# Turning the output weights for the router with six transposing DMAs instead of TensorE transposes

## The chip, the cores and the metric

The kernel runs on one core of a Trainium2 chip. The metric is the time of one execution in microseconds of the device. Three runs of the kernel before gave 1300.38, 1301.32 and 1308.1 us; the median, 1301.32 us, is the time before.

## What is computed

The reference is an attention between tokens and a small state, a gated MLP on its result, and a top-1 mixture of eight experts on the result of that. Cut to what matters:

```python
a  = softmax(scale * x @ state^T);   xread = a @ state      # per batch b (8) and head (8)
a2 = softmax(scale * state @ x^T);   sread = a2 @ x
x  = concat(xread, sread)                                   # 8 x (512 + 32) = 4352 rows of 512
h  = sigmoid(x @ w_gate) * (x @ w_val)                      # 512 -> 1536
x  = h @ w_out                                              # 1536 -> 512
logits = x @ moe2_w_gate                                    # 512 -> 8
e = argmax(logits); p = softmax(logits)[e]
out = p * relu(x @ w1[e]) @ w2[e]                           # 512 -> 1024 -> 512
```

The first three weights come as float64, which the kernel turns into float32 with integer operations; every product of two matrices is made of three float16 matmuls over high and low parts.

## The kernel before

The token rows of the first MLP are worked off in eight blocks of 512 tokens, one for each batch b (`token_block`), then come the 256 state rows, then the expert tiles of 128 rows (37 of them, `expert_tile`, L826), for which each row goes to its expert's list in DRAM. The hidden width of 1536 is cut into twelve groups of 128 (fc = 0 to 11, `NFC`), or six pairs (`NFP`).

In a block the work has two parts. First twelve steps of `gate_val` make the hidden activations (L618 to L620). Then four output rounds, j = 0 to 3, one for 128 tokens each (`mlp_out`, L669), add up twelve groups of three matmuls of 128x512 (L674 to L676) with the output weights `wout[:, fc, l]` (l = 1 the high, l = 0 the low part). At fc = 3, at fc = 7 and at its end a round calls `mid()`, which runs what a table has for that numbered slot: 25, 26, 27 are those of round 0, 28 to 30 of round 1, 31 to 33 of round 2, 34 to 36 of round 3. In these slots stand pieces of the next block's attention (L317 transposes, L330, L349, L390, L397, L408), of its state weights (L440, six times, in every second slot, copied out by ScalarE at L447 and VectorE at L448) and, in block 0 only, `router_weights`, in slots 25 to 31 and 33. Behind each slot a step of a background queue runs.

The router does not read the rows of the MLP's result. It multiplies the hidden activations with `gw`, which is w_out times the router's weights, made once in block 0: `gsum` (L979), its maximum (L985), then `gw` (L991, L992). For that product the output weights have to be turned, so that the 512 columns of a group lie on the partitions.

The output weights are ready late. `conv_wout` scales them group by group in block 0: ScalarE rounds a group into a buffer `junk`, VectorE writes the low part (L293, called at L546) and copies the high part (L547). The buffers `junk`, `wt`, `g` and `ls` share one pair of buffers (tag "g" of `tmp`).

The large buffers (`big`, five of 4 KB per partition) hold the raw output weights (twelve loads, L514), then the expert weights (L565). `conv_experts` takes these as 64 parts of 512 KB: each is loaded, its absolute maximum taken (by VectorE at L581 for w1, by ScalarE at L585 for w2), and eight parts later it is loaded again, scaled, split and written back to DRAM (L592). Input loads are L256 and L207. All of them are issued by SyncE (SP).

TensorE's order is that in which the code is written; in this part of the program the orders of the other engines and of SP come from a scheduler. Each engine, and SP's queue, works off its list in order, and waits at an instruction whose operands or buffers aren't ready. A buffer is given to a new tile when its last reader is done.

Of the kernel before, what the change touches and what calls it, by code (L numbers as in the profile page):

```python
# [10 lines left out]
F16 = mybir.dt.float16  # L11
I32 = mybir.dt.int32
AF = mybir.ActivationFunctionType
ALU = mybir.AluOpType
AX = mybir.AxisListType
# [3 lines left out]
P = 128  # L19
# [6 lines left out]
def attention_moe_router_kernel(  # L26
# [24 lines left out]
    nc = tc.nc  # L51
# [5 lines left out]
    NE, _, F2 = w1.shape  # L57
    NDC = DM // P
    NFC = DF // P
# [26 lines left out]
    NFP = NFC // 2  # L86
# [12 lines left out]
    ident = const.tile([P, P], F16, name="ident", tag="ident")  # L99
# [17 lines left out]
    g2p = const.tile([P, NDC, 2 * NE], F16, name="g2p", tag="g2p")  # L117
    gsum = const.tile([P, NFC, NE], F32, name="gsum", tag="gsum")
# [4 lines left out]
    def tl(shape, dt=F32, name="t", bufs=None, pool=None):  # L123
        kw = {} if bufs is None else {"bufs": bufs}
        return (pool or tiny).tile(shape, dt, name=name, tag=name, **kw)

    def pow2_scale(m, k, nm, lim=40, inv=True, bufs=None):

        n = m.shape[1]
        a = tl([P, n], I32, nm + "a")  # L130
        s = tl([P, n], I32, nm + "s", bufs)
        nc.vector.tensor_scalar(a, m.bitcast(I32), EXPO, EXPO, ALU.bitwise_and, ALU.bitwise_xor)
        nc.vector.tensor_scalar(
            s, a, float((128 + lim) * ONE), float((k - 1) * ONE), ALU.min, ALU.add
        )
        if not inv:
            return s.bitcast(F32), None
        c = tl([P, n], I32, nm + "c", bufs)
        nc.vector.tensor_scalar(c, s, -1.0, float(254 * ONE), ALU.mult, ALU.add)
        return s.bitcast(F32), c.bitcast(F32)  # L140
# [21 lines left out]
    tmp = mlp.enter_context(tc.tile_pool(name="tmp", bufs=2))  # L162
    big_p = mlp.enter_context(tc.tile_pool(name="big_p", bufs=5))
# [5 lines left out]
    wout = wpool.tile([P, NFC, 2, DM], F16, name="wout", tag="wout")  # L169
    x1s = wpool.tile([P, NDC, B * NS], F32, name="x1s", tag="x1s")  # L170

    def at_ps(shape, dt=F32):
        return at_p.tile(shape, dt, name="at", tag="at")
# [4 lines left out]
    def spread(m):  # L178

        n = m.shape[1]  # L180
        ps = at_ps([P, n, P])
        for i in range(n):
            nc.tensor.matmul(
                ps[:, i], m[:, i:i + 1].to_broadcast([P, P]), identf, start=True, stop=True
            )
        return ps

    def all_max(ps, nm):
        r = tl([P, ps.shape[1]], name=nm)
        nc.vector.tensor_reduce(r, ps, axis=AX.X, op=ALU.max)  # L190
        return r
# [92 lines left out]
    def pair(v, h16, l16, s=None, inplace=False):  # L284

        if inplace:
            nc.scalar.activation(v, v, AF.Copy, scale=s)  # L287
        if s is None or inplace:
            nc.scalar.copy(h16, v)  # L289
            nc.gpsimd.tensor_tensor(l16, v, h16, op=ALU.subtract)  # L290
        else:
            nc.scalar.activation(h16, v, AF.Copy, scale=s)
            nc.vector.scalar_tensor_tensor(l16, v, s, h16, op0=ALU.mult, op1=ALU.subtract)  # L293
# [661 lines left out]
    def router_weights():  # L955

        wt = {}
        for k in range(NFC + 1):
            if k < NFC:
                pt = at_ps([P, 2, NDC, P], F16)  # L960
                for l in range(2):
                    for c in range(NDC):
                        nc.tensor.transpose(
                            pt[:, l, c], wout[:, k, 1 - l, c * P:(c + 1) * P], ident
                        )
                wt[k] = tmp.tile([P, 2, NDC, P], F16, name="wt", tag="g")
                nc.vector.tensor_copy(wt[k], pt)
            if k > 0:
                pg = at_ps([P, 2, NE])
                w = wt.pop(k - 1)  # L970
                for c in range(NDC):
                    nc.tensor.matmul(
                        pg.rearrange("p l e -> p (l e)"), w[:, 0, c], g2p[:, c],
                        start=(c == 0), stop=False,
                    )
                    nc.tensor.matmul(
                        pg[:, 0], w[:, 1, c], g2p[:, c, 0:NE], start=False, stop=(c == NDC - 1)
                    )
                nc.vector.tensor_reduce(  # L979
                    gsum[:, k - 1], pg.rearrange("p l e -> p e l"), axis=AX.X, op=ALU.add  # L980
                )
            if k % 2 == 1:
                yield
        m = tl([P, 1], name="gm")
        nc.vector.tensor_reduce(  # L985
            m, gsum.rearrange("p f e -> p (f e)"), axis=AX.X, op=ALU.max, apply_absolute_value=True
        )
        yield
        r = all_max(spread(m), "gr")
        s, i = pow2_scale(r, 14, "gs")  # L990
        pair(gsum, gw[:, :, 0, 0], gw[:, :, 0, 1], s)  # L991
        nc.vector.tensor_copy(gw[:, :, 1, 0], gw[:, :, 0, 0])  # L992
        nc.vector.tensor_tensor(inv_g, inv_g, i, op=ALU.mult)
        yield
# [30 lines left out]
    def token_block(b):  # L1025
# [36 lines left out]
        if b == 0:  # L1062

            rw = router_weights()
            for slot in (25, 26, 27, 28, 29, 30, 31, 33):
                at(slot, lambda: next(rw, None))
# [102 lines left out]
    n = B * NS  # L1169
# [181 lines left out]
```

## Time and profile before

| | before |
|---|---|
| median of three runs | 1301.32 us |
| profiled execution: run, span | 1309.01 us, 1307.2 us |
| TensorE busy, share of the span | 1142.4 us, 87% |
| VectorE, ScalarE, GpSimd busy | 816.9, 589.8, 331.3 us |
| mean granted TensorE clock | 0.936 |
| router weights: first transpose, first matmul of block 1 | 174.76 us, 238.04 us |

The times of a trace count from the start of its span. A row of the order of time gives start, duration, engine, source line, operation, output and input tiles, and in brackets how long the engine had been idle and who ended that. The rows that matter stand below.

### The profile page before, as it was taken

What the parts mean: (1) busy time and instruction counts of PE and PEld (TensorE: products, weight loads), DVE (VectorE), ACT (ScalarE), POOL (GpSimd) and SP (SyncE); (2) the same over time, 40 slices, a digit from 0 to 9 for tenths busy, and PEclk for the clock granted to TensorE, in tenths of its full rate; (3) what the DMA queues carried; (4) which work ended last, traced back from release to release, by engine and by line L of the source; (5) the groups of instructions that cost most, each with busy time, mean ns of one, the idle gap of its engine ahead of it and who ended that gap; (6) DMA issues with size and microseconds to landing.
All of it is one profiled execution on the core that took longest, in us unless ns stands there. A gap on an engine that the chain in (4) does not pass through costs nothing.

```text
span 1307.2 us, 23292 instructions
## 1 busy us (share of the span) xinstructions
PE 1142.4 (87%) x8855; PEld 644.1 (49%) x8855; DVE 816.9 (62%) x1918; ACT 589.8 (45%) x963; POOL 331.3 (25%) x273
## 2 busy tenths in 40 slices
PE   3366659889889899799899999999999999999995
PEld 2222225444344444334444444486777766666773
DVE  7778877677768678686767574333644444444442
ACT  3666652576585785686785744121111111111110
POOL 1253200233252451351540714131110000000110
PEclk9577779899899999899899999999999999999998
DMA  7404420185576766476765300027322277879347
GB/s 249 165 33 146 161 85 6 48 276 182 194 242 217 258 224 252 162 255 228 267 212 187 122 2 34 1 105 229 125 60 62 53 243 237 290 198 383 89 122 230
DMA packets 118803, 216.71 MB, mean 166 GB/s; under 512 B 61215, under 2 KB 69407, under 8 KB 115360
## 3 DMA queue, kind: packets, MB, share of 16 engines
q1 hardware_dynamic: 113008, 197.07, 45.5%
q0 software_dynamic: 5680, 18.11, 3.6%
q8 instruction: 72, 1.18, 0.4%
q14 instruction: 43, 0.35, 0.1%
HBM read 259.35 MB, written 54.88 MB: 240 GB/s over the span
## 4 chain that ended last, share of the span: by engine, by line
PE 45%; DVE 18%; DMA 15%; ACT 12%; issue 6%; SPq 3%; POOL 1%; POOLq 0%; DVEq 0%; ACTq 0%
DMA big<-in_moe_w_dram 10%; PE mm L836 9%; PE mm L839 4%; PE mm L857 4%; PE mm L858 4%; PE mm L856 4%; PE mm L620 3%; PE mm L618 3%; PE mm L619 3%; PE mm L674 3%; PE mm L675 3%; PE mm L676 3%; DMA out_dram<-g,meta 2%; ACT big L287 2%; ACT big L585 1%
## 5 line engine op out<-in xcount | busy, mean ns | idle before, releaser
L850 ACT ACTIVATE acth<-v 128x256 f16<-128x256 f32 x148 | 61.8, 417 | 323.9 <-DVE v L849 302.3
L836 PE MATMUL mm<-big,wgv 128*128 128x256 f16 x1184 | 199.3, 273 | 0.4 <-DMA wgv<-w_d 0.4
L839 PE MATMUL mm<-big,wgv 128*128 128x128 f16 x1184 | 197.4, 219 | 0.0
L618 PE MATMUL mm<-aT,M 128*128 128x512 f16 x384 | 156.7, 408 | 42.0 <-ACT M L447 22.5
L631 POOL TENSOR_TENSOR actl<-g,acth 128x512 f16<-128x512 f32 (+1 forms) x108 | 127.7, 1185 | 181.2 <-ACT acth L630 180.5
L620 PE MATMUL mm<-aT,M 128*128 128x512 f16 x384 | 156.7, 408 | 13.2 <-DVE M L448 7.5
L674 PE MATMUL mm<-wout,acth 128*128 128x512 f16 x408 | 159.6, 391 | 8.8 <-DVE wout L547 6.8
L675 PE MATMUL mm<-wout,acth 128*128 128x512 f16 x408 | 158.9, 389 | 0.0
L676 PE MATMUL mm<-wout,actl 128*128 128x512 f16 x408 | 158.5, 389 | 0.0
L619 PE MATMUL mm<-aT,M 128*128 128x512 f16 x384 | 156.7, 408 | 0.0
L625 DVE SCALAR_TENSOR_TENSOR g<-mm,g 128x512 f32<-128x512 f32 (+1 forms) x108 | 70.9, 658 | 88.4 <-PE mm L620 42.0
L836 PEld LDWEIGHTS <-wgv 128*128 128x128 f16 x1184 | 115.8, 98 | 18.2 <-DMA wgv<-w_d 0.9
L864 POOL DMA_INDIRECT out_dram<-g,meta x37 | 36.2, 978 | 341.5 <-DVE g L861 304.5
L839 PEld LDWEIGHTS <-wgv 128*128 128x128 f16 x1184 | 115.8, 98 | 4.0
L849 DVE TENSOR_REDUCE v<-mm 128x256 f32<-128x512 f32 x148 | 101.4, 686 | 19.2 <-PE mm L839 18.2
L851 DVE SCALAR_TENSOR_TENSOR actl<-v,acth 128x256 f16<-128x256 f32 x148 | 62.9, 425 | 69.9 <-ACT acth L850 66.8
L290 POOL TENSOR_TENSOR big<-big 128x1024 f16<-128x1024 f32 x32 | 68.2, 2131 | 108.5 <-ACT big L289 96.5
L776 POOL DMA_INDIRECT rows_d<-xrow,rri x34 | 36.4, 1070 | 215.8 <-DVE kg L715 64.9
L630 ACT CAST acth<-g 128x512 f16<-128x512 f32 (+1 forms) x108 | 63.8, 591 | 53.0 <-DVE g L625 52.8
L861 DVE TENSOR_SCALAR g<-mm,meta,slot_inv 128x512 f32<-128x512 f32 x33 | 26.7, 810 | 95.6 <-PE mm L858 95.6
L624 ACT ACTIVATE g<-mm,sgf 128x512 f32<-128x512 f32 (+1 forms) x108 | 71.0, 659 | 24.6 <-PE mm L620 22.1
L448 DVE SCALAR_TENSOR_TENSOR M<-mm,M 128x512 f16<-128x512 f32 x96 | 62.5, 683 | 22.6 <-ACT M L447 22.6
(297 smaller groups left out, 2183.8 us busy)
## 6 DMA issues: line engine op xcount, KB each, us to landing
wgv<-w_d SPq DMA_DIRECT2D x59, 2048.0 KB
big<-in_moe_w_dram SPq DMA_DIRECT2D x128, 512.0 KB
wout<-w_d SPq DMA_DIRECT2D x19, 2048.0 KB
w_d<-big SPq DMA_DIRECT2D x64, 512.0 KB
xb<-in_x_dram SPq DMA_DIRECT2D x60, 128.0 KB
big<-in_moe_w_out_dram SPq DMA_DIRECT2D x12, 512.0 KB
wgv<-in_moe_w_gate_dram SPq DMA_DIRECT2D x3, 1024.0 KB
wgv<-in_moe_w_val_dram SPq DMA_DIRECT2D x3, 1024.0 KB
```

The source lines that it names most:

```text
L618: nc.tensor.matmul(ps[k], w[0], v[0], start=(i == 0), stop=False)
L619: nc.tensor.matmul(ps[k], w[0], v[1], start=False, stop=False)
L620: nc.tensor.matmul(ps[k], w[1], v[0], start=False, stop=(i == len(parts) - 1))
L624: mark["sig"] = nc.scalar.activation(g, ps[0], AF.Sigmoid, scale=sg[:, fc:fc + 1])
L625: nc.vector.scalar_tensor_tensor(g, ps[1], 2.0 ** -v_sh, g, op0=ALU.mult, op1=ALU.mult)
L631: nc.gpsimd.tensor_tensor(lo, g, h, op=ALU.subtract)
L674: nc.tensor.matmul(po, hj, wout[:, fc, 1], start=(fc == 0), stop=False)
L675: nc.tensor.matmul(po, hj, wout[:, fc, 0], start=False, stop=False)
L676: nc.tensor.matmul(po, lj, wout[:, fc, 1], start=False, stop=(fc == NFC - 1))
L836: nc.tensor.matmul(ph[:, i], w1s[:, c, 0, f:f + P], t[:, :, c], start=(c == 0), stop=False)
L839: nc.tensor.matmul(ph[:, i, 1], w1s[:, c, 1, f:f + P], t[:, 0, c], start=False, stop=(c == NDC - 1),)
L849: nc.vector.tensor_reduce(v, ph.rearrange("p i l q -> p i q l"), axis=AX.X, op=ALU.add)
```

## The change

The transposes on TensorE, their copies out of PSUM by VectorE and the tiles `wt` in the pair of "g" buffers are taken out. In their place six DMAs, issued by SP, each turn a pair of groups with both parts (128 partitions by 2048 float16, 512 KB) from `wout` into a large buffer. Two are issued in slot 25, one more ahead of each of the next four pairs; the router matmuls read the large buffers directly. The matmuls and the sums of the product stay as they were (new lines L976, L980 for L972, L976, and L983 for L979); those of pair n stand in slot 26 + n, where before the first group's stood in slot 25.

```diff
     def router_weights():
 
         wt = {}
-        for k in range(NFC + 1):
-            if k < NFC:
-                pt = at_ps([P, 2, NDC, P], F16)
-                for l in range(2):
-                    for c in range(NDC):
-                        nc.tensor.transpose(
-                            pt[:, l, c], wout[:, k, 1 - l, c * P:(c + 1) * P], ident
-                        )
-                wt[k] = tmp.tile([P, 2, NDC, P], F16, name="wt", tag="g")
-                nc.vector.tensor_copy(wt[k], pt)
-            if k > 0:
+
+        def turn(m):
+            if m < NFP:
+                wt[m] = big_p.tile([P, 2, 2, NDC, P], F16, name="big", tag="big")
+                nc.sync.dma_start_transpose(
+                    out=wt[m].rearrange("p k l c f -> p (k l c) f"),
+                    in_=wout[:, 2 * m:2 * m + 2].rearrange("p k l d -> p (k l d)"),
+                )
+
+        turn(0)
+        turn(1)
+        yield
+        for n in range(NFP):
+            turn(n + 2)
+            for i in range(2):
                 pg = at_ps([P, 2, NE])
-                w = wt.pop(k - 1)
+                w = wt[n][:, i]
...
-            if k % 2 == 1:
+            if n < NFP - 1:
                 yield
```

On TensorE, in round 0 behind fc 3, the transposes L963 of two groups and the router matmuls of the first group (`wt` is the copied transpose, `g2p` the router's weights) stood between an attention transpose and the matmuls of fc 4. Before:

```order
L317 MATMUL at<-ident,xn 128x128
L963 LDWEIGHTS wout
L963 MATMUL at<-ident,wout 128x128
...
L972 LDWEIGHTS wt
L972 MATMUL at<-g2p,wt 128x16
L976 LDWEIGHTS wt
L976 MATMUL at<-g2p,wt 128x8
...
L674 LDWEIGHTS acth
L674 MATMUL mm<-wout,acth 128x512
```

Now the same place, down to the router matmuls of the first pair, which read a large buffer and stand behind fc 7 and the state weights:

```order
L317 MATMUL at<-ident,xn 128x128
L674 LDWEIGHTS acth
L674 MATMUL mm<-wout,acth 128x512
...
L440 LDWEIGHTS bdT
L440 MATMUL mm<-wgv,bdT 32x512
...
L976 LDWEIGHTS big
L976 MATMUL at<-g2p,big 128x16
```

The sixteen transposes and eight router matmuls left the place; fc 4 follows the attention transposes directly.

On SP, behind the twelve loads of the raw output weights (`in_moe_w_dram` are the expert weights, `in_x_dram` and `in_state_dram` inputs):

```order
 L514 DMA big<-in_moe_w_out_dram 128x1024 x12
-L565 DMA big<-in_moe_w_dram 128x1024
-L256 DMA xb<-in_x_dram 128x256 x4
-L565 DMA big<-in_moe_w_dram 128x1024 x3
-L565 DMA big<-in_moe_w_dram 128x2x512
-L256 DMA xb<-in_x_dram 128x256 x4
+L256 DMA xb<-in_x_dram 128x256 x8
+L962 DMA_TRANSPOSE big<-wout 128x16x128 x2
+L565 DMA big<-in_moe_w_dram 128x1024
+L962 DMA_TRANSPOSE big<-wout 128x16x128
+L565 DMA big<-in_moe_w_dram 128x1024
+L962 DMA_TRANSPOSE big<-wout 128x16x128 x3
```

The first five expert loads stood ahead of the second input load; now two stand between the transposing DMAs and the third behind the last of them.

On VectorE, at the end of the conversions (L293 and L547 write `wout`; `gsum` is the router product, `em` an expert maximum):

```order
 L547 COPY wout<-junk 128x512
 L293 SCALAR_TENSOR_TENSOR wout<-wout,osc,junk 128x512
-L967 COPY wt<-at 128x1024
+L983 TENSOR_REDUCE gsum<-at 128x8
+L448 SCALAR_TENSOR_TENSOR M<-mm,M 128x512
 L547 COPY wout<-junk 128x512
-L581 TENSOR_REDUCE em<-big 128x1 x4
-L967 COPY wt<-at 128x1024
-L979 TENSOR_REDUCE gsum<-at 128x8
-L601 TENSOR_REDUCE ea<-em 128x1 x2
```

Ahead of the last conversion's copy a sum of the router product and a state weight copy have taken the place of a `wt` copy, and the four expert maxima that followed it are spread out behind.

## Rows read from the trace of the kernel before

**Rows 1.** The page: span and TensorE's busy time, share and instructions.
```profile
span 1307.2 us, 23292 instructions
PE 1142.4 (87%) x8855; PEld 644.1 (49%) x8855; DVE 816.9 (62%) x1918; ACT 589.8 (45%) x963; POOL 331.3 (25%) x273
```
**Rows 2.** Stages: length, busy us of PE, PEld, DVE, ACT, POOL; granted clock, DMA, GB/s.
```profile
174.96:181.91 6.95, 0.86 (x16) 0.68 (x13) 6.78 (x14) 5.12 (x8) 0.00 (x0) 0.91 0.00 0
...
192.00:238.04 46.04, 42.83 (x487) 23.57 (x484) 32.05 (x91) 13.20 (x24) 2.52 (x2) 1.00 0.02 5
...
173.90:180.70 6.80, 1.92 (x33) 1.74 (x31) 5.57 (x12) 5.34 (x8) 0.00 (x0) 1.00 0.00 0
180.70:187.50 6.80, 5.58 (x28) 2.00 (x36) 6.61 (x10) 1.92 (x4) 0.00 (x0) 0.50 0.64 199
```
**Rows 3.** PE's waits, 160 to 245 us: total us, times, longest us.
```profile
PE at L972 <- DVE wt L967: 11.5, 4, 6.1
```
**Rows 4.** PE in order of time: start, us, line, tiles, count, idle before.
```profile
174.76 1.06 PE L963 MATMUL at<-ident,wout 128*128 128x128 f16 x16
181.91 0.19 PE L972 MATMUL at<-g2p,wt 128*128 128x16 f16 x1 [6.10 <-DVE wt L967]
...
182.15 0.59 PE L674 MATMUL mm<-wout,acth 128*128 128x512 f16 x1
...
187.36 0.90 PE L440 MATMUL mm<-wgv,bdT 64*32 64x512 f16 x24
188.19 0.62 PE L963 MATMUL at<-ident,wout 128*128 128x128 f16 x8
188.65 0.17 PE L972 MATMUL at<-g2p,wt 128*128 128x16 f16 x1
...
191.78 0.18 PE L972 MATMUL at<-g2p,wt 128*128 128x16 f16 x1 [2.33 <-DVE wt L967]
...
192.00 0.38 PE L674 MATMUL mm<-wout,acth 128*128 128x512 f16 x1
192.21 0.38 PE L675 MATMUL mm<-wout,acth 128*128 128x512 f16 x1
...
209.25 0.18 PE L972 MATMUL at<-g2p,wt 128*128 128x16 f16 x1 [2.36 <-DVE wt L967]
...
238.04 0.38 PE L618 MATMUL mm<-aT,M 128*128 128x512 f16 x1
```
**Rows 5.** DVE in order of time, at the end of the conversions.
```profile
177.34 0.29 DVE L547 COPY wout<-junk 128x512 f16<-128x512 f16 x1
...
181.18 0.68 DVE L967 COPY wt<-at 128x1024 f16<-128x1024 f16 x1
181.78 0.28 DVE L547 COPY wout<-junk 128x512 f16<-128x512 f16 x1
```
**Rows 6.** SP's queue in order of time, and the stage of the expert loads.
```profile
181.49 5.54 SPq L565 DMA_DIRECT2D big<-in_moe_w_dram  x5
187.12 26.99 SPq L207 DMA_DIRECT2D st<-in_state_dram  x16
242.15 18.52 SPq L256 DMA_DIRECT2D xb<-in_x_dram  x8
...
181.00:191.00 10.00, 7.54 (x68) 3.20 (x68) 6.34 (x11) 3.98 (x9) 0.00 (x0) 0.67 0.78 252
```
**Rows 7.** L819: ns of one on SP (least, median, most); one of them; its stage.
```profile
L819 SPq DMA_TRANSPOSE big<-rows_d x41: 1242/1269/7444, 875.2 to 1294.4; - x41
...
939.93 1.27 SPq L819 DMA_TRANSPOSE big<-rows_d  x1
...
940.00:943.00 3.00, 3.00 (x27) 1.97 (x25) 2.23 (x5) 0.99 (x3) 0.00 (x0) 1.00 0.44 90
```
**Rows 8.** The chain of waits in order of time: two expert loads, start and us.
```profile
399.36 4.19 DMA big<-in_moe_w_dram
...
638.89 8.18 DMA big<-in_moe_w_dram
```

More of the change, by code (lines that the diff above doesn't have):

```diff
@@ L957, in router_weights @@
         wt = {}
-        for k in range(NFC + 1):
-            if k < NFC:
-                pt = at_ps([P, 2, NDC, P], F16)
-                for l in range(2):
-                    for c in range(NDC):
-                        nc.tensor.transpose(
-                            pt[:, l, c], wout[:, k, 1 - l, c * P:(c + 1) * P], ident
-                        )
-                wt[k] = tmp.tile([P, 2, NDC, P], F16, name="wt", tag="g")
-                nc.vector.tensor_copy(wt[k], pt)
-            if k > 0:
+        def turn(m):
[11 more added lines that the diff above has]
+            for i in range(2):
                 pg = at_ps([P, 2, NE])
-                w = wt.pop(k - 1)
+                w = wt[n][:, i]
                 for c in range(NDC):
                     nc.tensor.matmul(
-                        pg.rearrange("p l e -> p (l e)"), w[:, 0, c], g2p[:, c],
+                        pg.rearrange("p l e -> p (l e)"), w[:, 1, c], g2p[:, c],
                         start=(c == 0), stop=False,
@@ L976, in router_weights @@
                     nc.tensor.matmul(
-                        pg[:, 0], w[:, 1, c], g2p[:, c, 0:NE], start=False, stop=(c == NDC - 1)
+                        pg[:, 0], w[:, 0, c], g2p[:, c, 0:NE], start=False, stop=(c == NDC - 1)
                     )
                 nc.vector.tensor_reduce(
-                    gsum[:, k - 1], pg.rearrange("p l e -> p e l"), axis=AX.X, op=ALU.add
+                    gsum[:, 2 * n + i], pg.rearrange("p l e -> p e l"), axis=AX.X, op=ALU.add
                 )
-            if k % 2 == 1:
+            if n < NFP - 1:
                 yield
```

## The prediction

> **What bounds the kernel now.** I read the page first: TensorE (PE) is busy 87% of a span of 1307.2 us [rows 1], so a change that only empties another engine gives nothing, and I looked for the stretch that the diff touches and for what ended PE's waits in it. The router weights are made in block 0, in its four output rounds (j = 0 to 3, twelve groups fc of three matmuls each), from the first transpose at 174.76 us to the first matmul of block 1 at 238.04 us [rows 4]. The table by stage shows PE nearly idle at first (0.86 us busy of 6.95) while VectorE (DVE) is full (6.78 of 6.95), and a granted clock that goes 1.00, then 0.50 after the idle time [rows 2]. The table of waits names the cause: PE waited 11.5 us in four places at L972 for DVE's copy L967 [rows 3]. The longest is 6.1 us. DVE's order shows why: the copy L967 at 181.18 stands behind the conversions of the output weights (L293, L547; L547 of group 7 is at 177.34, that of the last group at 181.78, so about 1.1 us for each) [rows 5]. The next waits are the same kind: 2.33 us until 191.78 and 2.36 us until 209.25 [rows 4], the copy being behind DVE instructions that themselves wait (the expert maxima L581, then a maximum that waits for ScalarE, which waits for expert loads).
>
> **The sum: what goes.** All of it is measured against the profiled execution (span 1307.2, run 1309.01 us); the median of the three runs, 1301.32, is 7.7 us lower, and as this stretch is early and short, I subtract the same microseconds from the median.
> - 96 transposes leave PE. Eight of them take 0.62 us with the last one's tail, and the next instruction starts 0.46 us after the first (188.19 and 188.65, [rows 4]); twelve eights are 5.5 us.
> - The four waits for L967: 11.5 us [rows 3].
> - The half clock. Between 182.15 and 187.36 the twelve matmuls of fc 4 to 7 take 0.43 us each; at 192.00 and 192.21 the same matmul takes 0.215 [rows 4]. The clock had been granted at 1.00 from 173.9 and fell at 180.7, after PE had stood idle for 4.9 of 6.8 us [rows 2]. Without that idle time I expect it to stay up: 2.6 us.
>
> Together 19.6 us, which I take as the most that can be won; twelve copies of 0.68 us [rows 5] leave DVE too, but DVE is only worth what PE waits for it.
>
> **The walk: what is in the way instead.** With the transposes gone, fc 4 of round 0 starts at 174.96. It now meets the conversions themselves: fc 6 and fc 7 need their L547, and the one at 177.34 (group 7) ends at 177.63 [rows 5]. So fc 7 ends near 178.3; then the 24 matmuls L440 (0.8) and the first router pair (0.4, both from the starts in rows 4) bring fc 8 to 179.5, against 192.00: 12.5 us ahead. The last conversion gets a little later, because the new order puts two L983 and one L448 ahead of its L547 and these wait for PE and ScalarE: I put its end at 182.4 instead of 182.06, so fc 11 waits 0.9 us. Then rounds 1 to 3 save eight more transpose groups (8 x 0.46 = 3.7) and two waits (2.36 [rows 4] and what is left of the 11.5 after 6.1, 2.33 and 2.36, 0.7): 3.1 us. 12.5 - 0.9 + 3.7 + 3.1 = 18.4 us.
>
> **The six DMAs.** They wait on SP for their pair of groups and for a buffer, and SP is free for them: its next work before was the five expert loads at 181.49 [rows 6], and ahead of the transposes stand input loads alone. No transpose out of on-chip memory is in the trace. The nearest rows are the 41 transposes of L819, out of DRAM and half as large (128x1024): median 1.27 us on SP, one of 7.44 at worst [rows 7]; in the three microseconds from 940.00, which begin with one issued at 939.93, 90 GB/s or 270 KB went by, that is all of its 256 KB. Doubled, 2.5 us of SP each, and my estimate is that they land 4 us (lower bound 3.1, as for the half size) after the start. I take the median, as the same operation with the same piece size (16 rows by 128) is issued. Pair 0 is issued at about 169, needed at 179; pair 5 is needed at about 200, and six in a row from 169 with T = 2.5 are through long before. In detail pairs 3, 4 and 5 wait for buffers: for the first pair to be used (179.5), for the first L581 (184) and for the second pair (184.4), so they are issued by 189.2 and are 8 us early or more. With T up to 4.8 us ((200 - 169 - 2) / 6) nothing is late.
>
> Behind them on SP stand the expert loads of block 0. Five were resident before the conversions ended and five more were issued from 181.49 [rows 6]; now only two are ahead, and the third is issued at about 189.6, when pair 5 is out. A load that the chain waited for took 4.19 us [rows 8], so it lands near 193.6; DVE asks for it (L581) near 192.5 and behind it stand the row maxima L680 and L685 of round 1, for which a later L440 waits. So about 1 us of DVE is late, which this stretch can swallow (DVE was busy 32.05 of the last 46.04 us [rows 2]), and the next loads come one after another. By the first matmul of block 1 SP must have caught up: before, its row of state loads ended at 214.11 (187.12 and 26.99) and the next input load went out at 242.15 [rows 6], so the lag is inside its slack. From block 1 on, the order of every engine is the same as before and the rest should be moved as one piece.
>
> I subtract 3.4 us from the 18.4 for what a walk leaves out: one stretch of half clock somewhere else (2.6, as above) and 0.8 for late expert loads. **15 us** are left: 1301.3 - 15 = 1286.3.
>
> **The rivals.**
> - *Loads late, part of the gain given back.* The longest load that the chain waited for took 8.18 us [rows 8]. If the third to eighth load of block 0 take 8 us instead of 4, DVE and ScalarE stand 4 us at each of two places in their order, with L685 and the copies L447 behind: 4 to 8 us back, 1290 to 1298, say 1293. For it: the loads now queue behind six transposes. Against it: the five that were queued together at 181.49 went by within the ten microseconds to 191, at 252 GB/s [rows 6], 2 us each.
> - *The gain is lost later.* Blocks 1 to 7 also wait for expert loads, and if the loads set their pace, an earlier start buys nothing: 1301, within 4 us. Against it: SP's idle stretch before 242.15 says that the loads wait for PE's progress there and not the other way round.
> - *Slow transposes (the other side).* SBUF as the source may be slower than DRAM. The place is the wait of the router matmuls in PE's fixed order; each microsecond of T over 4.8 costs 6 us, as six stand in a row, so at T = 7.3 the gain is gone. At twice the worst row, T = 14.9, the cost is 6 x 10.1 - 15 = 46 us: 1347. For it: no row shows this source. Against: the median of 41 rows. The Trainium skill speaks for this rival ("VectorE: DVE Perf Modes", section "The three transpose paths"): it gives 1309 ns for one 128x128 block through the DMA against 390 ns on TensorE, and advises TensorE where the result may go to PSUM. By that figure, as an estimate, a DMA of sixteen blocks takes 20.9 us and the kernel 6 x 16.1 - 15 = 82 us more. The trace does not agree for the DRAM source: eight blocks took 1.27 us of SP [rows 7], where the page's figure would make 10.5.
>
> **How the numbers follow.** The forecast, 12 to 20 us won, gets 0.60; late loads 0.22; gain lost later 0.08; slow transposes 0.10. About 1% (13 us) is what a measurement of this kernel can tell from no change. Of the forecast's 0.60 the part under 13 us, 0.06, is within 1%, so faster by over 1% is 0.54. Late loads and a later loss are within 1%, 0.30, and so are slow transposes with T between 5 and 9.5 us, 0.02, and the 0.06: 0.38. Slower by over 1% needs T over 9.5: 0.08. The low end is 1301.3 less the 19.6 and 1.7 for a better clock elsewhere: 1280. The high end takes in the late loads and the lost gain up to no change: 1303. Outside are the slow transposes and a few hundredths below.
>
> **What would show it.** In the profile after: no wait of PE at the router matmuls for DVE, and none for a transposing DMA; the clock at 1.00 from 174 to 187; fc 8 of round 0 near 180; the first matmul of block 1 near 220 to 223; the transposes at about 2.5 us each on SP; the distance from the first matmul of block 1 to the end unchanged. Wrong would be: a PE wait ended by the transposing DMA, expert loads that end long waits of DVE or ScalarE between 190 and 215, or a block 1 that starts early and a block 2 that does not.

## The result, and the profile after

| | before | after |
|---|---|---|
| median, range of four runs each | 1303.55 us (1300.38 to 1308.1) | 1282.13 us (1278.23 to 1285.3) |
| profiled execution: run, span | 1309.01, 1307.2 us | 1282.37, 1280.6 us |
| first conversion of `wout` to first matmul of block 1 | 165.75 to 238.04: 72.3 us | 162.88 to 216.18: 53.3 us |
| first matmul of block 1 to the end of the span | 1069.2 us | 1064.4 us |

The ratio is 0.9838, 95% interval [0.9806, 0.9871]: 1.6% or 21.4 us faster. Measured once more beside other kernels, the change took 1279.79 us, ratio 0.9831 [0.9781, 0.9881]. The forecast was 1286.3 us, 15 us faster, with a range of 1280 to 1303.

The page after, beside [rows 1]: span, busy us, share of the span and instructions of each engine.

```profile
span 1280.6 us, 23091 instructions
PE 1125.5 (88%) x8759; PEld 635.9 (50%) x8759; DVE 803.5 (63%) x1906; ACT 588.3 (46%) x963; POOL 331.9 (26%) x273
```

Over the whole span PE is busy 16.9 us less, but a part of that lies outside the stretch that the change touches: two profiles of the kernel before differ by 7.3 us in it (1142.4 and 1135.1). So here is PE in the stretch alone, from the first conversion of `wout` to the first matmul of block 1 (columns as in [rows 2]), before and after:

```profile
165.75:238.04 72.29, 57.66 (x601) 30.58 (x602) 52.04 (x126) 27.16 (x46) 4.63 (x4) 0.90 0.13 41
```

```profile
162.88:216.18 53.30, 48.28 (x504) 24.38 (x505) 43.48 (x114) 26.39 (x46) 4.70 (x4) 0.94 0.64 164
```

Of the 19.0 us that went there, 9.4 were busy time (transposes, and matmuls at half clock) and 9.6 idle time. PE's waits from 160 to 245 us (total us, times, longest): one of before that [rows 3] does not show, then all of after:

```profile
PE mm L674 <- DVE wout L547: 6.8, 1, 6.8
```

```profile
PE mm L674 <- DVE wout L547: 8.5, 4, 7.1
PE at L743 <- DVE roh L736: 3.6, 1, 3.6
PE at L976 <- DVE gsum L983: 0.6, 1, 0.6
```

The 11.5 us for the copies are gone. At the router matmuls only 0.6 us are left, for the sum that frees a PSUM buffer, and none for a transposing DMA. The first two lines of after are not for this product: PE waits for the conversions, 7.1 us of it at the very first one, and, once block 1 has begun, for L736. The conversions themselves now cost PE 8.5 us where they had cost 6.8; that and the 0.6 are the part of the 11.5 that is not won. The stages of [rows 2], as the profile after has them:

```profile
174.96:181.91 6.95, 6.47 (x81) 3.00 (x81) 6.90 (x14) 3.08 (x6) 0.00 (x0) 1.00 1.10 208
...
173.90:180.70 6.80, 5.96 (x78) 2.62 (x78) 6.70 (x15) 3.45 (x6) 0.00 (x0) 1.00 1.10 201
180.70:187.50 6.80, 6.80 (x78) 3.43 (x75) 6.76 (x19) 2.85 (x6) 0.00 (x0) 1.00 1.11 243
```

In the 6.95 us in which PE had worked for 0.86 us it now works for 6.47, and the granted clock stays at 1.00 (2.4 GHz) where it had gone to 0.50 (1.2 GHz). The times count from the start of the span, and the conversions begin 2.87 us earlier here (162.88 against 165.75). DVE is as full as before: PE no longer depends on its next copy. PE in order of time after, beside [rows 4]:

```profile
171.04 0.38 PE L674 MATMUL mm<-wout,acth 128*128 128x512 f16 x1
...
174.26 0.38 PE L674 MATMUL mm<-wout,acth 128*128 128x512 f16 x1 [0.47 <-DVE wout L547]
...
175.77 0.18 PE L976 MATMUL at<-g2p,big 128*128 128x16 f16 x1
...
176.19 0.38 PE L674 MATMUL mm<-wout,acth 128*128 128x512 f16 x1
...
178.77 0.38 PE L674 MATMUL mm<-wout,acth 128*128 128x512 f16 x1 [0.48 <-DVE wout L547]
...
216.18 0.38 PE L618 MATMUL mm<-aT,M 128*128 128x512 f16 x1
```

These are fc 4, fc 7, the first router matmul, fc 8, fc 11 and block 1's first matmul. SP's queue after, beside [rows 6], and the group of the transposing DMAs (ns of one on SP: least, median, most; us to landing):

```profile
166.10 3.99 SPq L962 DMA_TRANSPOSE big<-wout  x2
170.14 0.58 SPq L565 DMA_DIRECT2D big<-in_moe_w_dram  x1
170.99 3.76 SPq L962 DMA_TRANSPOSE big<-wout  x1
...
176.36 8.30 SPq L962 DMA_TRANSPOSE big<-wout  x3
184.76 0.53 SPq L565 DMA_DIRECT2D big<-in_moe_w_dram  x1
...
L962 SPq DMA_TRANSPOSE big<-wout x6: 1571/2070/3978, 166.1 to 182.2; - x6
...
DMA to landing us min/median/max: 4.1/5.1/6.2
```

The three rows of the six span 16.05 us of SP, 2.7 us each; without the short gaps between two issues in one row it is 15.1 us, 2.5 each. The first pair was issued at 166.1 and used at 175.77, the last one was issued at 182.2.

### The profile page after: what moved, and what is told of

Read it like the earlier page. It is cut to its first block, busy times and chain, and to the rows that moved or that the text cites. A ratio compares the mean times of both kernels' runs of the same rounds, so it can differ in the third digit from the quotient of the medians.

```text
span 1280.6 us, 23091 instructions
## 1 busy us (share of the span) xinstructions
PE 1125.5 (88%) x8759; PEld 635.9 (50%) x8759; DVE 803.5 (63%) x1906; ACT 588.3 (46%) x963; POOL 331.9 (26%) x273
## 4 chain that ended last, share of the span: by engine, by line
PE 49%; DVE 15%; DMA 15%; ACT 10%; issue 5%; SPq 4%; POOL 1%; POOLq 0%; DVEq 0%; ACTq 0%
DMA big<-in_moe_w_dram 9%; PE mm L836 9%; PE mm L839 4%; PE mm L856 4%; PE mm L857 4%; PE mm L858 4%; PE mm L618 4%; PE mm L620 4%; PE mm L619 4%; PE mm L674 2%; PE mm L675 2%; PE mm L676 2%; DMA out_dram<-g,meta 2%; ACT big L585 1%; DVE big L293 1%
## 5 line engine op out<-in xcount | busy, mean ns | idle before, releaser
L618 PE MATMUL mm<-aT,M 128*128 128x512 f16 x384 | 155.5, 405 | 43.0 <-ACT M L447 22.9
L674 PE MATMUL mm<-wout,acth 128*128 128x512 f16 x408 | 157.7, 386 | 9.5 <-DVE wout L547 8.5
L675 PE MATMUL mm<-wout,acth 128*128 128x512 f16 x408 | 157.4, 386 | 0.0
L625 DVE SCALAR_TENSOR_TENSOR g<-mm,g 128x512 f32<-128x512 f32 (+1 forms) x108 | 70.8, 657 | 79.5 <-PE mm L620 39.1
L618 PEld LDWEIGHTS <-M 128*128 128x128 f16 x384 | 39.4, 103 | 75.5 <-ACT M L447 25.9
```

The lines of the kernel that those rows point to most:

```text
L618: nc.tensor.matmul(ps[k], w[0], v[0], start=(i == 0), stop=False)
L625: nc.vector.scalar_tensor_tensor(g, ps[1], 2.0 ** -v_sh, g, op0=ALU.mult, op1=ALU.mult)
L674: nc.tensor.matmul(po, hj, wout[:, fc, 1], start=(fc == 0), stop=False)
L675: nc.tensor.matmul(po, hj, wout[:, fc, 0], start=False, stop=False)
```

## The experiments

Below, "the stretch" is the time from the first conversion of the output weights (L293 on `wout`) to the first matmul of block 1 (L618), and "the rest" is from there to the end of the span, each in the profiled execution. "Over the change" compares medians with 1282.13 us.

**TensorE transposes, but one slot ahead.** The groups are transposed by TensorE and copied by DVE into the large buffers, a pair ahead of its use:

```diff
-                nc.sync.dma_start_transpose(out=wt[m]..., in_=wout[:, 2 * m:2 * m + 2]...)
+                for i in range(2):
+                    pt = at_ps([P, 2, NDC, P], F16)
...
+                            nc.tensor.transpose(
+                                pt[:, l, c], wout[:, 2 * m + i, l, c * P:(c + 1) * P], ident
+                            )
+                    nc.vector.tensor_copy(wt[m][:, i], pt)
...
-        turn(1)
...
-            turn(n + 2)
+            turn(n + 1)
```

> The changed kernel with TensorE transposes again: each pair of groups is turned on TensorE one slot ahead of its router matmuls and copied by VectorE into a large buffer; no transposing DMA. Theory A (the waits made the loss: the copy stood behind the conversions because its buffer was one of the two that the conversions use, and the router matmuls of the same slot needed it at once): the waits at the router matmuls fall from 11.5 us to under 3, the clock stays up from 174 to 187, and of the 21 us about 12 remain won: 1289 to 1294 us. What is missing against the change is 5.5 us of transposes on TensorE and a few us of copies on VectorE. Theory B (the work itself had to leave TensorE and VectorE): the waits come back in another place, under 4 us won: 1299 to 1304 us.

It took 1291.31 us (1287.38 to 1296.31), ratio 0.9918 [0.9891, 0.9946], within theory A's 1289 to 1294. In PE's waits for the stretch what is left for the copies is the first line, and from 174 to 187 us the granted clock is 1.00 (second line), as theory A has it:

```profile
PE at L979 <- DVE big L969: 1.5, 2, 1.3
...
174.00:187.00 13.00, 10.21 (x120) 5.45 (x120) 12.86 (x26) 4.46 (x7) 0.00 (x0) 1.00 0.13 42
```

and block 1 begins at 224.37, the conversions at 163.31: a stretch of 61.1 us. So 11 of the 19 us of the stretch are won without a DMA, by letting the copy be late without PE standing behind it. The edit moves the transposes a slot ahead and also takes the copies out of the pair of buffers that the conversions use; which of the two does it was not separated. The other 8 are 5.8 us of PE's busy time in the stretch (54.1 against 48.3) and 2.0 of its idle time (7.0 against 5.0). By the next experiment 5.0 of it are the transposes; that the idle time comes of the copies on DVE is likely, but not shown.

**The DMAs, and the transposes left on PE.** The change with the 96 transposes added back into PSUM, where nothing reads them:

```diff
             turn(n + 2)
+            for i in range(2):
+                pt = at_ps([P, 2, NDC, P], F16)
+                for l in range(2):
+                    for c in range(NDC):
+                        nc.tensor.transpose(
+                            pt[:, l, c], wout[:, 2 * n + i, l, c * P:(c + 1) * P], ident
+                        )
```

> The changed kernel with its six DMAs, and beside them the 96 TensorE transposes of before once more, in the slots of the router matmuls; nobody reads or copies their results. It prices TensorE's part alone. If TensorE sets the pace of this stretch, as both theories say, 96 x 0.057 = 5.5 us more than the changed kernel: 1286 to 1289 us, and the first matmul of block 1 comes 5 to 6 us later than in the profile after. If VectorE (rows maxima, expert maxima) sets the pace instead, less than 2 us more.

1288.93 us (1286.83 to 1289.37), ratio 0.9897 [0.9863, 0.9931]; the stretch is 58.3 us (165.43 to 223.75), 5.0 longer than with the change. The group of the added transposes (ns of one) and one lot of two groups in PE's order of time:

```profile
L976 PE MATMUL at<-ident,wout x96: 216/219/230, 179.1 to 203.6; 128*128 128x128 f16 x96
...
179.08 1.07 PE L976 MATMUL at<-ident,wout 128*128 128x128 f16 x16
```

The transposes themselves cost 5.0 us in the stretch against the forecast 5.5. The medians say 6.8, within their intervals.

**Each DMA twice.** Every pair is turned twice into the same tile (one line, `for _ in range(2):`, ahead of the DMA).

> The changed kernel with each transposing DMA issued twice into the same tile; the second waits until the first has landed. It doubles the suspected cost, the time of a transposing DMA in SP's queue: from the 4 to 5 us to landing of one and about 2 us of issue, 6 to 7 us a pair. By the prediction's price (nothing up to 4.8 us a pair, then 6 us for each us) this costs 7 to 13 us against the changed kernel: 1289 to 1295 us, as waits of TensorE at the router matmuls for the DMA or as waits of VectorE and ScalarE for expert loads behind it. The rival, that the DMAs have far more room because the scheduler puts the later readers further back, says under 3 us: below 1286 us.

1286.8 us (1284.97 to 1288.07), ratio 0.9878 [0.9843, 0.9914]: 4.7 over the change, between the two expectations. The twelve DMAs took 8.21 + 4.47 + 17.35 us of SP, 2.5 each or 5.0 a pair with the gaps between them (4.7 without), about the 4.8 up to which the prediction saw nothing late. The second DMA of a pair did wait for the first to land (the third on SP waits for the semaphore that the first one raises, the fourth for that of the second), but so SP takes two pairs by turns: the two first ones start at 169.32 and 171.74, the second one of pair 0 at 173.36. So a pair costs SP less than the 6 to 7 us expected. The stretch is 58.6 us (166.10 to 224.65), 5.3 longer than with the change. Two of PE's waits in it, then an expert maximum of DVE, then PE behind it:

```profile
PE at L349 <- DVE sT L336: 2.4, 1, 2.4
PE at L977 <- DMA big<-wout: 1.3, 2, 0.8
```

```profile
187.95 1.22 DVE L581 TENSOR_REDUCE em<-big 128x1 f32<-128x1024 f32 x1 [2.85 <-DMA big<-in_moe_w_dram]
189.09 0.68 DVE L336 SCALAR_TENSOR_TENSOR sT<-at,sT 128x512 f16<-128x512 f32 x1
```

```profile
189.82 0.56 PE L349 MATMUL at<-ident,sT 128*128 128x128 f16 x7 [2.43 <-DVE sT L336]
```

The direct wait for the DMA is 1.3 us; the prediction's price, 6 x (5.0 - 4.8), gives 1.2, but without the gaps it gives nothing, so that the two agree is chance. The longer wait came by the other way that the prediction had as a rival: an expert load behind the transposes on SP is late, DVE stands 2.85 us for it, and L336 behind it on DVE is what PE wants next (2.43 us). Behind this wait the granted clock is halved, which lengthens six output matmuls from 0.215 to 0.43 us, another 1.3 us:

```profile
191.60:194.90 3.30, 2.98 (x23) 1.33 (x24) 3.30 (x9) 2.19 (x5) 0.00 (x0) 0.50 1.23 270
```

**Each DMA four times** (`range(4)`).

> The change with each transposing DMA issued four times into the same tile. With the DMA issued twice, one took 1.88 us of SP at the median, so a pair should take 4 x 1.9 = 7.6 us. Theory A (the price of the prediction: nothing late up to 4.8 us a pair, then 6 us for each us): 6 x 2.8 = 17 us over the change, 1296 to 1303, with waits of PE for a transposing DMA at the router matmuls of 10 us and more in sum. Theory B (the router matmuls have slack, only the expert loads behind on SP are late, as most of the cost was when it was issued twice): 1286 to 1293, DVE's waits for expert loads grow, PE's waits for the transposing DMA stay under 4 us.

1320.42 us (1309.71 to 1323.59), ratio 1.0118 [1.0048, 1.0187]: slower than before, 38.3 over the change and above both expectations. The 24 DMAs took 56.3 us of SP, 2.35 each and 9.4 a pair (52.4 us, 8.7 a pair, without the gaps between them); I had put 7.6, from the median of one instead of the mean. The first eight on SP, and the stage in which they ran (1.09 is the mean busy share of the DMA engines):

```profile
167.93 18.08 SPq L963 DMA_TRANSPOSE big<-wout  x8
...
168.00:186.00 18.00, 9.64 (x64) 3.97 (x62) 11.15 (x23) 8.63 (x13) 0.00 (x0) 0.78 1.09 212
```

PE's waits for them in order of time, each with the first output matmul behind it:

```profile
186.35 0.20 PE L977 MATMUL at<-g2p,big 128*128 128x16 f16 x1 [8.06 <-DMA big<-wout]
186.80 0.59 PE L674 MATMUL mm<-wout,acth 128*128 128x512 f16 x1
...
208.07 0.20 PE L977 MATMUL at<-g2p,big 128*128 128x16 f16 x1 [11.84 <-DMA big<-wout]
208.52 0.59 PE L674 MATMUL mm<-wout,acth 128*128 128x512 f16 x1
...
225.83 0.19 PE L977 MATMUL at<-g2p,big 128*128 128x16 f16 x1 [7.69 <-DMA big<-wout]
226.28 0.59 PE L674 MATMUL mm<-wout,acth 128*128 128x512 f16 x1
```

The waits add up to 27.6 us; the price of the prediction, 6 x (9.4 - 4.8), is 27.6, or 23.6 without the gaps, so the size is right and the agreement to the decimal is chance. They are three, at pairs 0, 2 and 4, and not six, because SP takes two pairs by turns and these become ready together. What the price lacked stands in the second line of each pair: behind every wait the matmuls run at half clock again (0.59 for one against 0.38; the stage 205 to 216 us has a granted clock of 0.59). 31 output matmuls at 0.43 instead of 0.215 us are 6.7 of the 10.7 us that are left. In the stretch, 90.8 us here, PE is idle 28.3 us longer than after the change and busy 9.2 us longer with the same matmuls. DVE's waits for expert loads are 8.0 us here, but as only 0.7 us of PE's longer idle time lies beyond the 27.6, little of the loss can be theirs.

**The first expert loads late, in the kernel before.** The kernel before with the first five expert loads held until the last conversion, to see whether the loads that the change moves had been in anyone's way:

```diff
+        held = []
...
+            if len(held) < 5:
+                with tc.issue_after(mark["wo"].ins):
+                    held.append(nc.vector.memset(v[:, 0, 0:1], 0.0))
```

> The kernel before, with its first five expert loads of block 0 held back until the conversions of the output weights are done (a one-column write of VectorE into each of the five buffers stands behind the last conversion, and the load waits for it). It does one side effect of the change alone: no expert load between the input loads from 137 to 158 us. In the profile after, the conversions began 2.9 us earlier than before, of which 0.9 were there at 66 us already. Theory: the loads delayed the second input load and what hangs on it; then the first L293 of the conversions comes 1.5 to 2.5 us earlier here too, against 165.75. Rival: chance of the run; then it stays within 0.9 us. The time as a whole: the five loads now come late, behind the last conversion, and VectorE's maxima and ScalarE's with them, so I expect 0 to 8 us slower than before, 1303 to 1311 us.

1304.35 us (1300.36 to 1309.13), ratio 1.0004 [0.998, 1.0028]: no difference, so the early loads were neither a help nor a burden to the total. The stretch is 74.1 us (164.66 to 238.75), somewhat longer than before; the late loads have DVE stand 3.76 us for the first of them. Its conversions began at 164.66, 1.1 us ahead of the first profile of before; the next two experiments show that this start moves by itself.

**The change once more**, with a profile of its own.

> The change once more, beside the others and with a profile of its own. If its time is what was measured first: 1279 to 1286 at the median. From the first conversion to the first matmul of block 1 it took 53.2 us in the first profile, against 72.3 before, and 1064.5 us from there to the end against 1069.3. Theory A (the gain lies in the stretch; what differs before and behind it is scatter from run to run): 53 to 56 us for the stretch, 1060 to 1066 for the rest, and the start of the conversions anywhere from 162.5 to 166. Theory B (the change moves work outside the stretch too): the conversions start at 162.5 to 163.5 again.

1279.79 us (1278.2 to 1280.23). First DVE's row of the first conversion and its last copy, then PE's fc 8, fc 11 and the first matmul of block 1:

```profile
165.53 2.74 DVE L293 SCALAR_TENSOR_TENSOR wout<-wout,osc,junk 128x512 f16<-128x512 f32 x2 [0.27 <-ACT junk L292]
...
181.74 0.28 DVE L547 COPY wout<-junk 128x512 f16<-128x512 f16 x1
```

```profile
179.49 0.38 PE L674 MATMUL mm<-wout,acth 128*128 128x512 f16 x1
...
182.08 0.38 PE L674 MATMUL mm<-wout,acth 128*128 128x512 f16 x1 [0.48 <-DVE wout L547]
...
218.76 0.38 PE L618 MATMUL mm<-aT,M 128*128 128x512 f16 x1
```

The conversions begin 2.65 us later than in the first profile of the change and the stretch is the same, 53.2 us. The rest is 1058.8 us against 1064.4, 1.2 below the range of theory A. In the main that theory holds: the stretch repeats, the parts ahead and behind it scatter. Ahead of it PE takes 77.4 us for the same 538 entries of the trace in the first profile and 82.2 in the second. One stage in which the clock differs is that from 140 to 150 us, in the first profile of the change, then in the second:

```profile
140.00:150.00 10.00, 6.47 (x69) 3.36 (x68) 8.20 (x15) 7.42 (x15) 3.31 (x2) 1.00 0.19 54
```

```profile
140.00:150.00 10.00, 6.92 (x65) 3.00 (x64) 8.64 (x16) 6.19 (x12) 3.31 (x2) 0.83 0.17 54
```

It is one program, and PE was granted 1.00 in one execution and 0.83 in the other. The two profiles of before fit: PE is busy 82.4 and 79.5 us ahead of conversions that begin at 165.75 and 164.20. The mean granted clock over all the time ahead, idle time included, goes the other way in the change's two profiles (0.74 and 0.83), and that the clock sets this start is not shown by an experiment.

**The kernel before once more**, for the same reason.

> The kernel before once more, with a profile of its own. In its first profile it took 72.3 us from the first conversion of the output weights to the first matmul of block 1 and 1069.3 us from there to the end; six kernels with changes in that stretch alone took 1056 to 1069 us for the rest. Theory A (the rest is scatter, the stretch is not): 71.5 to 74 us for the stretch, and a rest of 1056 to 1068, mostly below the first. Theory B (the rest of the kernel before is really longer, by the 5 us that the first two profiles differ): 1068 to 1071 again.

1300.34 us in one run. PE's wait at the router matmuls, the first conversion, then fc 8 of round 0 and the first matmul of block 1:

```profile
PE at L972 <- DVE wt L967: 11.4, 4, 6.3
```

```profile
164.20 2.74 DVE L293 SCALAR_TENSOR_TENSOR wout<-wout,osc,junk 128x512 f16<-128x512 f32 x2 [0.27 <-ACT junk L292]
```

```profile
189.19 0.38 PE L674 MATMUL mm<-wout,acth 128*128 128x512 f16 x1
...
235.23 0.38 PE L618 MATMUL mm<-aT,M 128*128 128x512 f16 x1
```

The wait repeats (11.4 us). The stretch is 71.0 us, 0.5 below what theory A allowed, and the rest 1063.3. Two profiles of each kernel give 71.7 and 53.3 us: 18.4 us of gain in the stretch, of which PE's idle time is 10.0 (14.6 against 4.6) and its busy time 8.4 (57.1 against 48.7). For the rest they give 1066.3 and 1061.6, with 6 us between two profiles of the same kernel; the seven other profiles run from 1056.0 to 1069.1. So the 3 us by which the medians differ more than the stretch (21.4 against 18.4) are not told apart from scatter.

**One DMA ahead instead of two.**

```diff
         turn(0)
-        turn(1)
...
-            turn(n + 2)
+            turn(n + 1)
```

> The change with one transposing DMA ahead of the pair in use instead of two. Theory A (two ahead is more than the landing time of 4.1 to 6.2 us needs, as pairs are some 8 us apart on PE): no wait of PE for a transposing DMA, one large buffer more for the expert loads; 1279 to 1285. Theory B (the second in flight is needed): PE waits for the DMA at the first matmul of pairs 1 to 5, 1 to 2 us each; 1286 to 1292.

1280.54 us (1278.28 to 1286.82), ratio 0.9855 [0.9798, 0.9911]: the same as the change. PE's waits at the router matmuls in the stretch:

```profile
PE at L975 <- DVE gsum L982: 0.9, 2, 0.5
PE at L975 <- DVE aT L392: 0.5, 1, 0.5
```

None is for a DMA. But the edit hardly moved the issues: SP made them at 168.71, 171.13, 175.98, 180.04, 183.71 and 185.99, against 168.74, 171.16, 173.63, 179.66, 183.78 and 185.45 in the second profile of the change, so only the third is much later, and in both runs three were issued ahead of the first use at 179.0. Whether a second one in flight is needed was not tested by this. The pairs are 3.5 to 4.5 us apart on PE (179.01, 183.52, 187.83 and so on), not 8 as expected. The stretch is 55.05 us (165.49 to 220.54), 1.8 longer than in either profile of the change, which the medians cannot resolve; why is open.

**Issued by ScalarE.** The same six DMAs from ScalarE's queue (`nc.scalar.dma_start_transpose`).

> The change with the six transposing DMAs issued from ScalarE's queue instead of SP's. Theory A (SP had room; an issue holds the engine that makes it): ScalarE loses some 2 us six times and stands in order for the buffers, the squares ahead of the conversions come late, PE waits for conversions; 1284 to 1292. Theory B (the expert loads behind the transposes on SP cost the change something): the loads go out earlier and DVE's 2.0 us of waiting for them go; 1278 to 1282.

1288.3 us (1275.76 to 1292.66), ratio 0.9865 [0.9815, 0.9915]; the stretch is 56.6 us (165.26 to 221.82), 3.3 longer than with the change. The median lies in theory A's range, but the six runs spread over 17 us, the interval overlaps that of the change, and the profile is of the slowest run, so only the stretch says that it is worse. One DMA, the rounding L292 behind it (no square, as the expectation calls it), and the last two roundings, in ScalarE's order of time; then the PE row that waits for them:

```profile
171.07 1.65 ACTq L962 DMA_TRANSPOSE big<-wout  x1
171.39 0.71 ACT L292 ACTIVATE junk<-wout,osc 128x512 f16<-128x512 f32 x1
...
180.69 1.33 ACT L292 ACTIVATE junk<-wout,osc 128x512 f16<-128x512 f32 x2 [1.07 <-DVE M L448]
```

```profile
183.11 0.59 PE L674 MATMUL mm<-wout,acth 128*128 128x512 f16 x1 [2.84 <-DVE wout L547]
```

The next rounding starts 0.32 us after the issue begins, so, against theory A, this issue does not hold ScalarE for its 1.65 us. But another queue changed the order: the last two conversions now stand behind the state weight copies L448, and PE waits 2.84 us for them, with the half clock behind (0.59 for the matmul). The profile names L448 as what released the last two roundings at 180.69; L448 ended at 180.45 and an issue that began at 179.00 ended at 180.59, so the issue is not ruled out there.

## Why the prediction was right, point by point

- **The cause.** Right: the wait for the copies and the half clock behind it. Taking away the wait, with the same transposes on PE and the same copies on DVE, shortens the stretch from 71.7 to 61.1 us. The 10.6 are near the terms for it: 11.5 + 2.6, less the 1.5 that is left of the wait and the 1.9 that the conversions then ask more (8.8 against 6.9).
- **The transposes.** 5.5 us forecast, 5.0 measured when they were put back.
- **The half clock.** The clock stayed at 1.00 from 173.9 to 187.5, as forecast. That it falls to half behind idle time of PE was seen again where the DMAs were issued four times (behind waits of 8.06, 11.84 and 7.69 us) and twice (0.50 from 191.6, behind 2.43 us).
- **The copies at 209.25.** The prediction has the waits behind the first one come of expert maxima. For the one that ended at 191.78 the chain of waits says so (an expert load, ScalarE's L585 at 189.79, then the copy L967 at 191.13). The copy at 208.51 stood on DVE behind block 1's `xT` (L293 at 207.00) instead. The price, 2.36 us, is not touched by this.
- **The walk.** It gave fc 8 of round 0 at 179.5, with conversions that begin at 165.75; in the profile with conversions at 165.53 it is at 179.49. The last conversion was put at 182.4 and its wait at 0.9 us; it ended at 182.02 and the wait was 0.48. Counted from the first conversion, fc 8 came 12.0 us earlier at the mean of two profiles each (26.25 and 24.99 us before, 13.31 and 13.96 after), where the walk had 12.5; from fc 8 to block 1 it was 6.4 (46.04 twice; 39.99 and 39.27), where it had 5.9. The walk's sum of 18.4 us is the mean of the pairs, 71.7 - 53.3. That the decimal agrees is luck, as the single pairs give 19.0 and 17.8.
- **The allowance.** This is the step that failed: 3.4 us taken off for what a walk leaves out, 2.6 for another half clock and 0.8 for late loads. Neither came. PE was granted 1.00 through the stretch from fc 3 or fc 4 on. DVE waited 2.0 us for expert loads there, and no wait of PE was behind it. So block 1 began at 216.18 and 218.76, ahead of the 220 to 223 that the prediction gave as its sign (in the first profile 2.87 us of that are the earlier start). Without the allowance the forecast is 1282.9, against 1282.13 and 1279.79 measured. Part of this closeness is luck: the base of 1301.32 lies 2.2 below the median of four runs, and the gain between the medians 3.0 above the walk's.
- **The DMAs.** 2.5 us of SP forecast, 2.7 measured with the gaps between them, and 2.6 in the second profile. They landed after 5.1 us at the median and 6.2 at most, where I had estimated 4; as the first pair was issued 9.7 us ahead of its use, this cost nothing. The last one was out by 184.7, and the third expert load followed at 184.76; I had put them at 189.2 and 189.6. 2.9 us of the difference are the earlier start of the conversions (in the second profile the load went out at 187.57); for the rest I had the pairs wait for buffers longer than they did.
- **Slow transposes.** 1309 ns for one block, as the Trainium skill has it ("VectorE: DVE Perf Modes", section "The three transpose paths"), does not hold here as a price for each block of a larger transfer: sixteen blocks landed 5.1 us after the start, so at most 0.32 us for each. What one block alone takes no run here shows. The advice that the prediction takes from the same page of the Trainium skill, TensorE where the result may go to PSUM (it stands in the section "Rules for kernel authors"), was no argument for this rival: here the transposes had to be copied out of PSUM (L967) for the router matmuls. The price of slowness was of the right size in its waits (1.3 and 27.6 us measured, 1.2 and 27.6 by the rule of 6 us for each us over 4.8, nothing and 23.6 without the gaps on SP) and too low in all, as it left out the half clock behind each wait and the loads on SP. On a line between the DMAs issued twice (5.0 us a pair, 4.7 lost) and four times (9.4 us, 38.3 lost) the gain of 21.4 us is used up at 7.2 us a pair; the prediction said 7.3, from a smaller gain and a lower price, two errors that cancel.
- **Loads late.** It was not what happened, but it was the right second limit: with SP's transposes doubled, the longer of the two waits came of it.
- **The rest moved as one piece.** Within the scatter of 6 us, yes. Block 2 began 97.2 and 92.3 us behind block 1 before, 94.6 and 92.2 after, so what was won ahead of block 1 was not lost there.

## What to carry to other kernels

Where PE stands in a fixed order behind a copy of a busy VectorE, the length of the copy says little: the wait is the copy's place in VectorE's queue, and the clock that falls behind the wait adds to it. Making the transposes a slot further ahead, into buffers of their own, won 10.6 of the 18.4 us; handing them to a queue that had room won the rest. Before a DMA is put on a shared queue, work out how much slower it may be before something is late, and look at what is queued behind it as well as at its own consumer.

## What the runs showed of the hardware

- A transposing DMA of 512 KB from on-chip memory to on-chip memory took 1.6 to 4.0 us of SP, and from ScalarE's queue 1.6 us at the median (1.3 to 1.7); it landed 3.9 to 6.2 us after its start in the two profiles of the change, and 3.7 us after it from ScalarE's queue. In the run with four of each, eight in a row took 18.08 us, 2.26 us each, which is 232 GB/s, with the DMA engines at a mean share of 1.09. As they wait there, from the third on, for one two ahead to land (4.2 us at the median), the runs do not tell whether the rate or this wait sets that pace.
- One program's clock differs from one execution to the next ahead of the stretch (1.00 and 0.83 from 140 to 150 us), and its conversions start up to 2.65 us apart. A single pair of profiles is no measure of such a difference: 26.6 us between the first two spans, of which 18.4 belong to the change by two pairs.
